# Attention with a bucket mask and two expert layers on one core: when two products of early attention units may be issued

## The chip, the cores and the metric

The program runs on one core of one Trainium2 chip. The metric is the device time of one execution in microseconds; lower is better. The kernel before took 711.56 us, the median of three runs (709.78, 711.56 and 711.82). Its profiled execution took 714.04 us.

## The reference

Attention comes first: two batches, eight heads, 768 positions, head dimension 64. Queries and keys are hashed with six random projections, and a position may only look at positions of its own bucket. Two expert layers follow, each 512 to 2048 to 512.

```
q_bits = (einsum(q, proj) > 0); k_bits = (einsum(k, proj) > 0)     # 6 bits a position
mask   = bucket(q_bits) == bucket(k_bits)
attn   = softmax(where(mask, q @ k.T / sqrt(D), -1e9))
x      = (attn @ v), heads joined                                  # 1536 x 512
h = x @ w_in;  g = where(h > 0, h, exp(min(h, 0)) - 1); x = g @ w_out
h = x @ w_in2; g = s * max(h, 0)**2 + b;                out = g @ w_out2
```

The weights arrive as 64-bit floats and are decoded on the chip. Most products are done with numbers split into a high and a low 16-bit half.

## The kernel before, in words

Attention is cut into 96 units. A unit is 128 query rows of one head against all 768 keys. The first 16 units (two groups of eight, one for each head pair and row chunk) are done in one way, the other 80 in another.

A unit of the first 16 goes through these steps. `u_s` (L384) puts the scores on TensorE in four products into a PSUM tile `s`. `u_soft` (L395 on VectorE, L397 on ScalarE) caps them, takes the smallest of each row and makes the exponentials, the tile `p`. `u_split` (L406) transposes `p` on TensorE into the PSUM tile `pT` by six transposes, and ScalarE copies it to `pt` (L409). `u_av` (L434) multiplies `pt` by the values in six products, which gather in one eighth of the PSUM tile `xacc`. The transposes and these products work on 32-bit floats. There is one buffer for `s`, two for `pT`. A group's eighth unit is followed by `u_norm`, which divides by the sums, splits into halves and transposes by DMA into `x`, the input of the expert layers. The later units split `p` on ScalarE and GpSimd (L416, L419), transpose it by DMA (`pt<-ph`, L421) and multiply in 18 products of 16 bits (L440).

Beside attention two other things run from the start. `w_stream` decodes the first expert layer's weights in 32 chunks of which the 16 of `w_in` come first: a load into one of three buffers `wraw` (L175), then three VectorE instructions L213, L214 and L216, then ScalarE, GpSimd or VectorE for the high and low halves. A load waits until L216 has emptied its buffer. And the four head pairs of the first batch are prepared one after the other: L280 to L315 split and transpose keys and queries, L340 (`pbit`, 18 products) makes the hash bits, L343 turns them into zeros and ones, L353 (`pone`) and L357 turn those into the mask's rows.

When both first groups are done, `moe1` begins with the first expert layer (`h` and `x2p`, L574, products of 128x256), and its products are dealt out between the attention units by a credit. The second batch's keys and queries are loaded when all weights of the first layer have been decoded. The second expert layer (`up2`, `down2`) fills the time from about 475 us.

The code is a list of operations with priorities. A scheduler places them in each engine's queue by its own idea of times, and each engine works through its queue in that order. `tc.issue_after(x)` tells the scheduler not to place the operations under it ahead of the instruction `x`; `pins` is the table of such instructions. A change in one place can thus move instructions on all engines later in the program.

Of the kernel before, what the change touches and what calls it, by code (L numbers as in the profile page):

```python
# [63 lines left out]
W_FROM = 3  # L64
HOLD = {(0, 2, "v"): 3, (0, 3, "v"): 4, (1, 0, "k"): 8, (1, 0, "q"): 9}
HOLD_E = []
LN2 = 0.6931471805599453


def model_kernel(tc, q, k, v, proj, w_in, w_out, w_in2, w_out2, s2, b2, sel, pop, eye, out):  # L70
    nc = tc.nc
# [3 lines left out]
    C = S // 128  # L75
# [19 lines left out]
    with ExitStack() as base:  # L95
# [68 lines left out]
        w_loads, pins = [], {}  # L164

        def behind(n):

            return tc.issue_after(w_loads[n]) if n is not None else nullcontext()
# [9 lines left out]
        def w_early(ch, x):  # L178
            t = xx[1].rearrange("p a t -> p (a t)").bitcast(I32)[:, 1024 * x:1024 * x + 1024]
            with behind(HOLD_E[x]):  # L180
                nc.sync.dma_start(out=t.rearrange("p (k n) -> p k n", k=ch[1].shape[1]), in_=ch[1])
            return ch, t.rearrange("p (n t) -> p n t", t=2)
# [47 lines left out]
        ident = const.tile([128, 128], F32, name="ident")  # L230
# [133 lines left out]
        def unit(u):  # L364
            b, r = divmod(u, C * H)
            c, h = divmod(r, H)
            if u < FC * H:
                c, h = h // (H // 2), H // 2 * c + h % (H // 2)
            return b, c, h, h // 2, h % 2

        def group(u):

            return u // H, u % H
# [4 lines left out]
        def u_s(u):  # L378
            b, c, h, hp, j = unit(u)
            p = ps_s[0].tile([128, S], F32, tag="s", name="s")  # L380
            for x, (w, m) in enumerate(((q1, k1), (q2, k2))):
                kf = m[b, hp][:, j].rearrange("p c t -> p (c t)")
                for a0, a1 in halves:
                    nc.tensor.matmul(p[:, a0:a1], w[b, hp][:, j, c, :], kf[:, a0:a1],  # L384
                                     start=(x == 0), stop=(x == 1))
            sps[u] = p

        def u_soft(u):
# [6 lines left out]
            nc.vector.tensor_scalar(f, sps.pop(u), CLAMP, None, op0=ALU.min, op1=ALU.min, accum_out=mx)  # L395
            (nc.gpsimd if U0 <= u < MXP else nc.vector).tensor_scalar(mx, mx, sm / (SQ * SQ), 10.0 * LN2, op0=ALU.mult, op1=ALU.add)  # L396
            nc.scalar.activation(out=f, in_=f, func=ACTF.Exp, scale=-sm / (SQ * SQ), bias=mx,  # L397
# [3 lines left out]
        def u_split(u, eng):  # L401
            f = pf.pop(u)
            if u < FC * H:
                p = ps_p[0].tile([128, S], F32, tag="s", name="pT")
                for cc in range(C):
                    nc.tensor.transpose(p[:, 128 * cc:128 * cc + 128], f[:, 128 * cc:128 * cc + 128], ident)  # L406
                o = ring.take("pt", [128, S], F32, "pt")
                if eng == "act":
                    nc.scalar.activation(out=o, in_=p, func=ACTF.Copy)  # L409
                else:  # L410
                    nc.vector.tensor_copy(out=o, in_=p)
                pt[u] = o
                return
            t = ring.take("ph", [128, 2, S], F16, "ph")
            if eng == "act":
                nc.scalar.activation(out=t[:, 0, :], in_=f, func=ACTF.Copy)  # L416
            else:
                nc.vector.tensor_copy(out=t[:, 0, :], in_=f)
            nc.gpsimd.tensor_tensor(out=t[:, 1, :], in0=f, in1=t[:, 0, :], op=ALU.subtract)  # L419
            o = ring.take("pt", [128, 2 * C, 128], F16, "pt")  # L420
            nc.sync.dma_start_transpose(out=o, in_=t.rearrange("p x s -> p (x s)"))  # L421
            pt[u] = o

        def u_av(u):
            b, c, h, hp, j = unit(u)
            gr, sl = group(u)
            if sl == 0:
                xacc[gr] = ps_x.tile([128, H, D], F32, tag="x", name="xacc")
            acc = xacc[gr][:, sl, :]
            o = pt.pop(u)  # L430
            if u < FC * H:
                vv = raws[b, hp, "v"].rearrange("p h (c d) -> p h c d", d=D)
                for cc in range(C):
                    nc.tensor.matmul(acc, o[:, 128 * cc:128 * cc + 128], vv[:, j, cc, :],  # L434
                                     start=(cc == 0), stop=(cc == C - 1))
                return
            vv = vHL[b, hp]
            for z, (x, y) in enumerate(((0, 0), (0, 1), (1, 0))):
                for cc in range(C):
                    nc.tensor.matmul(acc, o[:, C * x + cc, :], vv[:, j, cc, y, :],  # L440
                                     start=(z == 0 and cc == 0), stop=(z == 2 and cc == C - 1))
# [76 lines left out]
        def attention():  # L518
            for i in range(-PRE, 0):
                for fn, a in sched.get(i, []):  # L520
                    fn(*a)
                yield
            while nxt["av"] < NU:
                if nxt["split"]:
                    u_split(nxt["split"].pop(0), SPLIT(nxt["s"]))
                u = nxt["av"]
                if u < nxt["s"] and u in pt and (nxt["s"] - u >= nxt["lag"] or nxt["s"] == NU):
                    u_av(u)
                    nxt["av"] += 1
                    if u % H == H - 1:  # L530
                        u_norm(u // H)
                        if u >= FC * H - 1:
                            done_chunks[0] = u // H + 1
                u = nxt["s"]
                if u < NU and u - nxt["av"] < nxt["lag"]:
                    if u == U0:
                        ring.use(p=[unp], ph=[un3], pt=[ptp])
                        nxt["lag"] = PT
                    u_s(u)
                    nxt["s"] += 1  # L540
                    yield
                    u_soft(u)
                    nxt["split"].append(u)
                    for fn, a in sched.get(u, []):
                        fn(*a)
                yield
# [305 lines left out]
        if True:  # L852
# [14 lines left out]
            for _ in att:  # L867
                n += 1
                if len(early) < len(HOLD_E) and len(w_loads) > HOLD_E[len(early)]:
                    early.append(w_early(co1[len(early)], len(early)))  # L870
# [155 lines left out]
```

## Time and profile before

| what | value |
|---|---|
| median of three runs | 711.56 us |
| profiled execution, own time | 714.04 us |
| its span on the core | 711.8 us |
| TensorE busy | 659.6 us, 93% |
| VectorE busy | 520.5 us, 73% |
| ScalarE busy | 416.3 us, 58% |
| GpSimd busy | 266.1 us, 37% |
| mean granted TensorE clock | 0.978 |

The profiled execution's time is 2.2 us longer than its span, and 2.5 us longer than the median of the runs. All instants below are counted from the start of the span. Busy shares are means over stages with different limits: from about 325 us on TensorE is busy almost without a gap, before that it isn't.

### The profile page before, as it was taken

To read this page: it belongs to the slowest core of one execution; us is meant where nothing else is said; L and a number is where in the kernel's file an instruction comes from. 1 tells how busy PE (TensorE), PEld (TensorE's weight loads), DVE (VectorE), ACT (ScalarE), POOL (GpSimd) and SP (SyncE) were. 2 spreads that over 40 slices of the span, in tenths; PEclk is the share of its full clock that TensorE was granted. 3 is DMA by queue.
4 is the path that set the end of the run, shared out by engine and by line. 5 is a ranking of instruction groups with operands and counts; after the bars stand their busy time and mean duration, and the time that the engine had idled before them with its cause. 6 is when DMAs were issued, how large, how long until landed. Compare 5 with 4: busy or idle time off the path is not lost.

```text
span 711.8 us, 15212 instructions
## 1 busy us (share of the span) xinstructions
PE 659.6 (93%) x6192; PEld 506.6 (71%) x6192; DVE 520.5 (73%) x893; ACT 416.3 (58%) x687; POOL 266.1 (37%) x211
## 2 busy tenths in 40 slices
PE   2598978879989999999999999999999999999998
PEld 0286857668767777888888988874444446888887
DVE  5779989998878568645644699339999626999730
ACT  2849768966778788656755333234545525555520
POOL 0136767776345469945855421311211200000000
PEclk9769999999999999999999999999999999999999
DMA  9965699999999669977668555014443000000100
GB/s 211 299 162 170 160 203 203 223 228 225 196 211 216 116 116 171 150 125 122 119 115 117 135 162 165 1 31 119 135 138 112 0 1 1 16 31 31 45 30 30
DMA packets 206805, 89.72 MB, mean 126 GB/s; under 512 B 171920, under 2 KB 203408, under 8 KB 206736
## 3 DMA queue, kind: packets, MB, share of 16 engines
q1 hardware_dynamic: 206144, 88.63, 57.4%
q8 instruction: 48, 0.79, 0.5%
q14 instruction: 21, 0.17, 0.1%
q10 hardware_dynamic: 592, 0.14, 0.1%
HBM read 43.13 MB, written 3.15 MB: 65 GB/s over the span
## 4 chain that ended last, share of the span: by engine, by line
PE 66%; DMA 10%; DVE 10%; ACT 7%; issue 5%; SPq 1%; POOL 1%; DVEq 0%; ACTq 0%; POOLq 0%
PE h L574 27%; PE y L818 15%; PE x2p L574 12%; DMA pt<-ph 6%; PE s L384 4%; PE xacc L440 3%; PE xacc L434 2%; DVE p L395 2%; ACT p L397 1%; PE pT L406 1%; ACT ph L416 1%; DMA q<-src 1%; DVE g L591 1%; DMA raw<-in_k 1%; ACT q L357 1%
## 5 line engine op out<-in xcount | busy, mean ns | idle before, releaser
L419 POOL TENSOR_TENSOR ph<-p,ph 128x768 f16<-128x768 f32 x80 | 134.6, 1686 | 79.2 <-ACT ph L416 44.3
L574 PE MATMUL h<-x,wih 128*128 128x256 f16 x768 | 131.3, 275 | 3.0 <-DVE g L591 1.5
L574 PE MATMUL h<-x,wi 128*128 128x512 f16 x576 | 124.5, 379 | 0.0
L395 DVE TENSOR_SCALAR_CACHE_REDUCE p<-s 128x768 f32<-128x768 f32 x96 | 91.0, 951 | 42.2 <-PE s L384 41.3
L397 ACT ACTIVATE p<-p,mx 128x768 f32<-128x768 f32 x96 | 89.2, 929 | 50.6 <-DVE mx L396 38.8
L818 PE MATMUL y<-wqh,a 128*128 128x256 f16 x672 | 110.3, 273 | 0.0
L818 PEld LDWEIGHTS <-a 128*128 128x128 f16 x1008 | 98.6, 98 | 11.7
L574 PE MATMUL h<-x,wil 128*128 128x256 f16 x384 | 105.4, 275 | 0.0
L574 PE MATMUL x2p<-gh,woh 128*128 128x256 f16 x384 | 104.1, 273 | 0.8 <-ACT gh L594 0.8
L574 PE MATMUL x2p<-gl,woh 128*128 128x256 f16 x384 | 104.5, 273 | 0.1
L574 PEld LDWEIGHTS <-wi 128*128 128x128 f16 x576 | 56.4, 98 | 67.7
L574 PE MATMUL x2p<-gh,wol 128*128 128x256 f16 x384 | 104.5, 273 | 0.0
L818 PE MATMUL y<-wql,a 128*128 128x256 f16 x336 | 91.1, 273 | 0.0
L384 PE MATMUL s<-k,q 128*128 128x512 f16 (+1 forms) x384 | 80.7, 335 | 8.0 <-DVE p L395 7.9
L574 PEld LDWEIGHTS <-wih 128*128 128x128 f16 x768 | 74.9, 99 | 15.2 <-issue 2.0
L574 PEld LDWEIGHTS <-woh 128*128 128x128 f16 x768 | 74.9, 98 | 11.6
L597 POOL TENSOR_TENSOR gl<-g,gh 128x512 f16<-128x512 f32 x48 | 59.0, 1229 | 61.0 <-ACT gh L594 60.7
L440 PE MATMUL xacc<-vv,pt 128*128 128x64 f16 x1440 | 57.6, 194 | 16.1 <-DMA pt<-ph 16.1
L416 ACT ACTIVATE ph<-p 128x768 f16<-128x768 f32 x80 | 66.7, 836 | 7.7 <-DMA pt<-ph 5.2
L440 PEld LDWEIGHTS <-pt 128*128 128x128 f16 x1440 | 53.5, 99 | 24.3 <-DMA pt<-ph 20.3
L610 DVE SCALAR_TENSOR_TENSOR g<-h,sbs,r 128x512 f32<-128x512 f32 x48 | 35.7, 745 | 23.6 <-ACT r L607 23.6
L384 PEld LDWEIGHTS <-q 128*128 128x128 f16 x384 | 34.5, 100 | 25.6 <-issue 10.8
(118 smaller groups left out, 1040.8 us busy)
## 6 DMA issues: line engine op xcount, KB each, us to landing
wraw<-in_moe_w_in SPq DMA_DIRECT2D x32, 512.0 KB, 3.9
wraw<-in_moe_w_out SPq DMA_DIRECT2D x32, 512.0 KB, 3.9
out<-y SPq DMA_DIRECT2D x10, 256.0 KB, 2.0
raw<-in_k SPq DMA_DIRECT2D x6, 384.0 KB, 4.8
raw<-in_q SPq DMA_DIRECT2D x6, 384.0 KB, 5.7
v<-in_v SPq DMA_DIRECT2D x4, 384.0 KB, 7.8
pt<-ph SPq DMA_TRANSPOSE x80, 4.1
x<-in_k SPq DMA_DIRECT2D x2, 384.0 KB, 5.0
```

The costliest lines, as they stand in the source:

```text
L357: nc.scalar.activation(out=o[r, j].rearrange("p c t -> p (c t)"), in_=p[r], func=ACTF.Relu, scale=sc, bias=pop_sb[r, x:x + 1])
L384: nc.tensor.matmul(p[:, a0:a1], w[b, hp][:, j, c, :], kf[:, a0:a1], start=(x == 0), stop=(x == 1))
L395: nc.vector.tensor_scalar(f, sps.pop(u), CLAMP, None, op0=ALU.min, op1=ALU.min, accum_out=mx)
L397: nc.scalar.activation(out=f, in_=f, func=ACTF.Exp, scale=-sm / (SQ * SQ), bias=mx, accum_out=sums[gr][:, sl:sl + 1])
L416: nc.scalar.activation(out=t[:, 0, :], in_=f, func=ACTF.Copy)
L419: nc.gpsimd.tensor_tensor(out=t[:, 1, :], in0=f, in1=t[:, 0, :], op=ALU.subtract)
L434: nc.tensor.matmul(acc, o[:, 128 * cc:128 * cc + 128], vv[:, j, cc, :], start=(cc == 0), stop=(cc == C - 1))
L440: nc.tensor.matmul(acc, o[:, C * x + cc, :], vv[:, j, cc, y, :], start=(z == 0 and cc == 0), stop=(z == 2 and cc == C - 1))
L574: nc.tensor.matmul(p, ws[a](kk), xs[b](kk), start=(kk == 0 and z == 0), stop=(kk == n_kk - 1 and z == 2))
L597: nc.gpsimd.tensor_tensor(out=gl, in0=t["g"], in1=gh, op=ALU.subtract)
L610: nc.vector.scalar_tensor_tensor(out=g, in0=p, scalar=sb["s"], in1=t["r"], op0=ALU.mult, op1=ALU.mult)
L818: nc.tensor.matmul(p, a[:, xa, kk, :], wq[y][:, WQ[n], kk, :], start=first and k == 0, stop=k == 3 * K2 - 1, skip_group_check=True)
```

## The change

Two operations get a place that they may not go ahead of. The first value product of unit 0 is placed behind the last transpose of unit 2, the first value product of unit 1 behind the last score product of unit 4. The other lines only keep these instructions in the table. Each group of six products gathers in one place of PSUM and so follows its first.

```diff
+HOLD_A = {0: ("pT", 2), 1: ("s", 4)}
...
-                    nc.tensor.matmul(p[:, a0:a1], w[b, hp][:, j, c, :], kf[:, a0:a1],
-                                     start=(x == 0), stop=(x == 1))
+                    pins["s", u] = nc.tensor.matmul(p[:, a0:a1], w[b, hp][:, j, c, :], kf[:, a0:a1],
+                                                    start=(x == 0), stop=(x == 1)).ins
...
-                    nc.tensor.transpose(p[:, 128 * cc:128 * cc + 128], f[:, 128 * cc:128 * cc + 128], ident)
+                    pins["pT", u] = nc.tensor.transpose(p[:, 128 * cc:128 * cc + 128], f[:, 128 * cc:128 * cc + 128], ident).ins
...
                 for cc in range(C):
-                    nc.tensor.matmul(acc, o[:, 128 * cc:128 * cc + 128], vv[:, j, cc, :],
-                                     start=(cc == 0), stop=(cc == C - 1))
+                    with tc.issue_after(pins[HOLD_A[u]]) if u in HOLD_A and not cc else nullcontext():
+                        nc.tensor.matmul(acc, o[:, 128 * cc:128 * cc + 128], vv[:, j, cc, :],
+                                         start=(cc == 0), stop=(cc == C - 1))
```

In the changed code the lines behind the first edit are numbered one or two higher: L384 becomes L385, L395 L396, L406 L407, L434 L436, L574 L576.

TensorE's queue before, from the end of unit 3's scores (`s_431`). `pt_317`, `pt_378` and `pt_429` belong to units 0, 1 and 2, `pT_422` and `pT_471` to units 2 and 3, `s_480` is unit 4's scores:

```order
L384 MATMUL s_431<-k21_189,q21_199 128x256
L434 MATMUL xacc_543<-v0_339,pt_317 128x64 x6
L434 MATMUL xacc_543<-v0_339,pt_378 128x64 x6
L406 MATMUL pT_422<-ident_109,p_395 128x128 x6
L384 LDWEIGHTS q10_177
L384 MATMUL s_480<-k10_168,q10_177 128x512
...
L384 MATMUL s_480<-k20_169,q20_179 128x256
L434 MATMUL xacc_543<-v0_400,pt_429 128x64 x6
L406 MATMUL pT_471<-ident_109,p_446 128x128 x6
L340 LDWEIGHTS pjkhl_134
```

The same place now:

```order
L385 MATMUL s_431<-k21_189,q21_199 128x256
L407 MATMUL pT_422<-ident_109,p_395 128x128 x6
L436 MATMUL xacc_543<-v0_339,pt_317 128x64 x6
L385 LDWEIGHTS q10_177
L385 MATMUL s_480<-k10_168,q10_177 128x512
...
L385 MATMUL s_480<-k20_169,q20_179 128x256
L436 MATMUL xacc_543<-v0_339,pt_378 128x64 x6
L436 MATMUL xacc_543<-v0_400,pt_429 128x64 x3
L407 MATMUL pT_471<-ident_109,p_446 128x128 x6
L341 LDWEIGHTS pjkhl_134
```

Unit 2's transposes went ahead of both value products, unit 4's scores ahead of unit 1's. Half of unit 2's value products now stand behind the hash bits and unit 5's scores.

VectorE's queue before, at the reduction of unit 4 (`p_495<-s_480`) and the hash bits of the third head pair (`bits_521`). `wx_327` and `wx_364` belong to two successive weight chunks:

```order
L346 COPY k23_409<-k23_409 64x768
L395 TENSOR_SCALAR p_495,mx_496<-s_480 128x768
L214 SCALAR_TENSOR_TENSOR wx_327<-wraw_288,wx_327 128x512
L396 TENSOR_SCALAR mx_496<-mx_496 128x1
L315 COPY q23_458<-q13_456 64x768 x2
L216 SCALAR_TENSOR_TENSOR wa_326<-wraw_288,wx_327 128x512
L213 TENSOR_SCALAR wx_364<-wraw_308 128x512
L343 TENSOR_SCALAR bits_521<-pbit_500 128x768
L214 SCALAR_TENSOR_TENSOR wx_364<-wraw_308,wx_364 128x512
```

And now:

```order
L347 COPY k23_409<-k23_409 64x768
L215 SCALAR_TENSOR_TENSOR wx_327<-wraw_288,wx_327 128x512
L396 TENSOR_SCALAR p_495,mx_496<-s_480 128x768
L217 SCALAR_TENSOR_TENSOR wa_326<-wraw_288,wx_327 128x512
L316 COPY q23_458<-q13_456 64x768 x2
L397 TENSOR_SCALAR mx_496<-mx_496 128x1
L214 TENSOR_SCALAR wx_364<-wraw_308 128x512
L215 SCALAR_TENSOR_TENSOR wx_364<-wraw_308,wx_364 128x512
L217 SCALAR_TENSOR_TENSOR wa_363<-wraw_308,wx_364 128x512
L344 TENSOR_SCALAR bits_521<-pbit_500 128x768
```

One decoding step now stands ahead of unit 4's reduction, and two more steps of the next chunk (before, behind the bits) stand ahead of the bits.

Later the queues differ too. TensorE's queue before, behind unit 22's scores (`s_1208`), where `h` is the first expert layer:

```order
L384 MATMUL s_1208<-k23_409,q23_458 128x512
L384 LDWEIGHTS q23_458
L384 MATMUL s_1208<-k23_409,q23_458 128x256
L574 LDWEIGHTS wih_154
L574 MATMUL h_1071<-x0_113,wih_154 128x256
```

And now:

```order
L385 MATMUL s_1208<-k23_409,q23_458 128x512
L385 LDWEIGHTS q23_458
L385 MATMUL s_1208<-k23_409,q23_458 128x256
L385 LDWEIGHTS q13_456
L385 MATMUL s_1256<-k13_408,q13_456 128x512
```

Unit 23's scores (`s_1256`) had 36 expert products ahead of them that now come behind. Counted over the whole queue, the expert products (L574) ahead of a unit's scores were 621 and are 591 for unit 48, 792 and 729 for unit 56, and 888 and 888 for unit 67; from there on TensorE's queue is the same in both.

## Rows read from the trace of the kernel before

**Rows 1.** The page, part 1: busy time, share of the span, instructions.
```profile
PE 659.6 (93%) x6192; PEld 506.6 (71%) x6192; DVE 520.5 (73%) x893; ACT 416.3 (58%) x687; POOL 266.1 (37%) x211
```
**Rows 2.** Stretches: length, busy us (count) by engine, granted clock, DMA share, GB/s.
```profile
34.00:49.00 15.00, 15.00 (x79) 12.16 (x78) 9.94 (x20) 6.89 (x12) 5.09 (x4) 0.50 0.87 197
49.00:176.00 127.00, 109.57 (x1168) 88.88 (x1165) 116.95 (x213) 100.33 (x174) 89.73 (x81) 0.97 0.90 197
100.00:275.00 175.00, 156.34 (x1881) 126.57 (x1880) 143.28 (x254) 139.01 (x239) 108.03 (x90) 0.99 0.99 193
205.00:245.00 40.00, 34.27 (x400) 26.50 (x399) 29.50 (x49) 33.44 (x54) 19.51 (x13) 1.00 0.94 177
245.00:275.00 30.00, 28.80 (x366) 23.51 (x365) 20.14 (x47) 25.15 (x43) 21.01 (x15) 1.00 0.77 140
```
**Rows 3.** Timeline of PE, 34 to 56 us: start, length, instructions, idle before, releaser.
```profile
35.69 5.22 PE L434 MATMUL xacc<-v,pt 128*128 128x64 f32 x24
40.70 1.49 PE L406 MATMUL pT<-ident,p 128*128 128x128 f32 x6
41.98 1.49 PE L384 MATMUL s<-k,q 128*128 128x512 f16 x4
43.26 2.66 PE L434 MATMUL xacc<-v,pt 128*128 128x64 f32 x12
45.72 1.49 PE L406 MATMUL pT<-ident,p 128*128 128x128 f32 x6
47.13 0.61 PE L340 MATMUL pbit<-k,pjkhl 128*32 128x512 f16 x2
...
52.32 1.45 PE L434 MATMUL xacc<-v,pt 128*128 128x64 f32 x12
...
55.84 0.81 PE L384 MATMUL s<-k,q 128*128 128x512 f16 x4 [1.42 <-DVE p L395]
```
**Rows 4.** Timeline of DVE, 39 to 50 us.
```profile
39.76 0.36 DVE L346 COPY k<-k 64x768 f16<-64x768 f16 x1
43.51 0.96 DVE L395 TENSOR_SCALAR_CACHE_REDUCE p<-s 128x768 f32<-128x768 f32 x1 [3.39 <-PE s L384]
...
45.18 1.12 DVE L315 COPY q<-q 64x768 f16<-64x768 f16 x2
46.33 0.69 DVE L216 SCALAR_TENSOR_TENSOR wa<-wraw,wx 128x512 int32<-128x512 int32 x1
...
49.18 0.96 DVE L343 TENSOR_SCALAR bits<-pbit 128x768 f16<-128x768 f32 x1 [1.44 <-PE pbit L340]
```
**Rows 5.** Timeline of ACT, 35 to 37 us.
```profile
35.70 0.94 ACT L397 ACTIVATE p<-p,mx 128x768 f32<-128x768 f32 x1 [0.23 <-DVE mx L396]
36.54 0.18 ACT L397 ACTIVATION_READ_ACCUMULATOR p<-p,mx 128x1 f32 x1
```
**Rows 6.** The stretch of one microsecond in which the granted clock rose.
```profile
48.00:49.00 1.00, 1.00 (x16) 0.42 (x8) 0.00 (x0) 0.79 (x2) 0.59 (x1) 0.55 0.73 193
```
**Rows 7.** Waits of DVE, 50 to 180 us: total us, times, longest.
```profile
DVE p L395 <- PE s L384: 5.2, 6, 1.5
DVE g L591 <- ACT e L584: 2.1, 1, 2.1
```
**Rows 8.** Waits of PE, 100 to 320 us.
```profile
PE xacc L440 <- DMA pt<-ph: 14.0, 13, 2.4
```
**Rows 9.** Timelines of DVE and PE at units 53, 56 and 67.
```profile
248.74 0.96 DVE L395 TENSOR_SCALAR_CACHE_REDUCE p<-s 128x768 f32<-128x768 f32 x1 [5.56 <-PE s L384]
252.84 0.81 PE L384 MATMUL s<-k,q 128*128 128x512 f16 x4
276.18 1.46 PE L384 MATMUL s<-k,q 128*128 128x512 f16 x8
```
**Rows 10.** The chain that ended last: start, us, what; an expert product's price.
```profile
178.18 3.63 DMA raw<-in_k
301.56 2.62 PE x2p L574 x24
```

## Prediction

> **What bounds the kernel now.** I read the page's busy shares first: TensorE 93%, VectorE 73% [rows 1]. Such a mean hides stages, so next came the table of stretches [rows 2]. Idle TensorE time is what an early change can win. Of the 175 us from 100 to 275 it is busy for 156.34, so idle for about 18.7 us; 14.0 us of idle time up to 320 us is value products waiting for the transposes by DMA [rows 8]. The stretch from 49 to 176 us belongs to VectorE: 116.95 of 127 us busy. There it decodes weights and does the reductions, and what it gains early it can hand on up to the end of the decoding, which is followed by the second batch's loads, on the chain at 178.18 us [rows 10].
>
> The change acts in 34 to 49 us. Here it is TensorE that has no gap: 15.00 us busy of 15, at a granted clock of 0.50, the lower of the two levels (1.2 GHz) [rows 2]. VectorE works 9.94 us of the 15. Its two waits are both for TensorE: 3.39 us for unit 4's scores and 1.44 us for the hash bits [rows 4]. The reason stands in TensorE's timeline: 24 records of value products for units 0 and 1 run from 35.69 to 40.70 us, 5.01 us, ahead of the transposes and scores on which the other engines wait [rows 3].
>
> **The change part by part.** It removes no instruction and adds none; it reorders. I walk TensorE's queue from 35.69 us with the spacings of [rows 3], all at 1.2 GHz.
>
> Unit 2's transposes come first now, and they need unit 2's exponentials, which ScalarE ends at 36.54 + 0.18 = 36.72 us [rows 5]. So TensorE idles some 1.1 us, until 36.8. Transposes 1.28 us (40.70 to 41.98), to 38.1. Unit 0's products half of 5.01, 2.5 us, to 40.6. Unit 4's scores 1.28 us, to 41.9, against 43.26 before: 1.4 us earlier. Unit 1's products 2.5 us, to 44.4; half of unit 2's products, half of 2.46 us, to 45.6; unit 3's transposes with the step to the bits 1.4 us (45.72 to 47.13), to 47.0. The hash bits begin at 47.0 instead of 47.13. The new gap of 1.1 us is paid by the 1.2 us of unit 2's products that were put behind. Those cost half as much at the higher level: a unit's 12 records take 2.66 us at the one and 1.45 us at the other [rows 3]. For 49 to 56 us that means some 0.6 us more work on TensorE, covered by the 1.42 us that it waits at 55.84 us for VectorE [rows 3]; if that cover went, 0.6 us would be lost.
>
> VectorE's queue in the same time: a decoding step fits behind the copy at 39.76 us, about 0.65 us; the reduction of unit 4 begins near 42.1 instead of 43.51. Behind it stand a decoding step, the copies (1.12 us), and three more decoding steps at 0.69 us each or a little less, since neighbours overlap [rows 4]. The queue is done at about 46.9 us and waits for the bits until 49.05. Waits: 1.4 + 2.2 = 3.6 us where 3.39 + 1.44 = 4.83 us were. The win is two decoding steps done, 1.2 to 1.4 us, plus 0.1 us from the earlier bits. I take 1.5 us of head start. The load buffer emptied by L216 is free near 43.7 instead of 47.0 us, so SP's next weight load goes 3.3 us earlier; SP's queue has nothing in front of it there. I cost it at nothing, since VectorE works on chunks loaded before it; its bounds are the 3.3 us by which it moves, to either side: that much earlier data, or that much delay to the value loads beside which it now runs.
>
> The clock decides how long all this runs at half speed. TensorE was busy without a gap from 34 us on and the clock rose only at about 48.9 (0.55 as the mean of 48 to 49) [rows 6], while the hash bits ran. These come at the same time in both orders, and so I leave the rise where it is. The Trainium skill, "TensorE: Matmul & The Clock Gate", Part 1, says that the moment of release is not the same from run to run, since the monitor isn't tied to the kernel's start; no run here shows that yet. By it, the rise could come earlier or later than 48.9 in either kernel, and neither the sum nor the order of the two changes in the mean. A later rise is priced among the rivals.
>
> What then happens to 1.5 us? From 49 to 176 us VectorE carries it, if its other waits stay: 5.2 us for scores and 2.1 us for an exponential of the expert layer [rows 7]. The second may vanish, since the expert work stands further back in the queue now. So the decoding's end comes 1.5 us earlier, up to 1.5 + 2.1 + 5.2 = 8.8 us at the very most. Behind it the order itself differs: unit 48's scores have 30 expert products less in front of them, unit 56's 63 less, unit 67's none less (counts in the change's section). One costs 2.62 / 24 = 0.109 us [rows 10], so TensorE has 6.9 us less behind it when it reaches unit 56 and makes that up between units 56 and 67. That stretch ran from 252.84 to 276.18 us [rows 9], with TensorE 96% busy, about 0.9 us idle [rows 2]. It will be 23.3 + 6.9 - 0.9 = 29.3 us long. Unit 56 must therefore come 6.0 us earlier just to break even, and 7.5 us earlier for the head start to arrive. For it speak the 5.56 us that VectorE waited at 248.74 for scores that stood behind expert products [rows 9], the ScalarE share of 205 to 245 us (33.44 of 40 us) from which 63 products' worth of activations now go behind, and the head start itself.
>
> Sum: 0 for TensorE up to 49 us, -1.5 us for VectorE handed on, later reordering about even. Against the profiled execution, 714.04 - 1.5 = 712.5 us, its span 711.8 - 1.5 = 710.3; that execution lies 2.5 us above the runs' median, and on the median's scale the forecast is 711.56 - 1.5 = 710.1 us.
>
> **The rivals.**
> *The later queue pays out more.* The waits for scores and for the exponential [rows 7] shrink by half, 3.6 us, and unit 56 comes early enough: 711.56 - 1.5 - 3.6 = 706.5 at the far end, 707.8 with two thirds of it. For it: the waits are for TensorE and ScalarE work that stood behind expert work. Against: TensorE's own waits are mostly for transposes by DMA [rows 8], which no order of products shortens.
>
> *Slower: TensorE starved at units 48 to 56.* The attention there is held by loads, ScalarE and DMA transposes [rows 2, 8], and the expert products that filled the gaps have been put behind. If unit 56 comes only 1.5 us earlier, the end moves by 6.0 - 1.5 = +4.5 us: 716.1. If it comes 4 us earlier: 713.6. It decides from 6.0 us downwards. For it: TensorE was idle 5.7 us of 205 to 245 already. Against: VectorE's long wait above.
>
> *The gap is what counts.* In 34 to 49 us TensorE was the one busy engine, and the change puts a gap of 1.1 us in. If nothing later has slack, 711.56 + 1.1 = 712.7. The Trainium skill, "Perfetto Trace Analysis", Identifying the Most-Contended Engine, reads it so: improve the engine with the most work, by the gaps on it. By that rule the time would be 712.7; the trace speaks against, as TensorE then waits 1.42 us for VectorE at 55.84.
>
> *The clock rises later.* If the low level lasts from 48.9 to the next gap at 54.4, that work, 5.5 us at most, takes twice as long: up to +4 us after the 1.42 us of cover, 715.6.
>
> *No effect.* The head start is used up by another wait, perhaps the loads: 711.6.
>
> **How the numbers follow.** Chances: forecast 0.38 (its own range 708.6 to 711.6), more paid out 0.22, starved 0.23, gap 0.06, clock later 0.04, no effect 0.07. A measurement of this kernel can tell some 0.3%, 2.1 us, from no change: faster is below 709.4, slower above 713.7. Faster: the second case nearly whole, 0.21, and the lower part of the first, 0.15: 0.36. Slower: most of starved, 0.20, of the clock, 0.04, and a little of the gap, 0.02: 0.26. Within: 0.38. Range: down to 706.8, where the second case ends but for some 0.06, and up to 714.8, past the middle of the starved case, with some 0.12 left out.
>
> **What would show it.** Right: unit 4's reduction near 42.1 us, unit 2's transposes at 36.8, the bits at 49.0, VectorE's two waits 3.6 us in sum, the loads of the second batch at 174.5 to 177 instead of 178.18, unit 56's scores at or before 245.4. Wrong: the clock rising anywhere else than about 48.9 us, the second batch's loads no earlier, or unit 56 later than 246.8 us with TensorE idle before it.

## The result: 1.1% slower, and the profile after

| | before | after |
|---|---|---|
| median of 4 runs, us | 711.69 (709.78 to 713.87) | 719.56 (718.15 to 720.40) |
| profiled execution, us: own time, span | 714.04, 711.8 | 719.76, 718.0 |
| TensorE idle in the span, us | 52.2 | 58.1 |

The ratio is 1.0108, with a 95% interval of 1.0074 to 1.0141. The forecast was 710.1 with a range up to 714.8: the sign is wrong. TensorE has the same work (659.6 before, [rows 1]); the span grew by 6.2 us, and its idle time by 5.9.

The page's first part, against [rows 1], and two stretches with the columns of [rows 2]:

```profile
PE 659.9 (92%) x6192; PEld 505.5 (70%) x6192; DVE 527.7 (73%) x893; ACT 415.5 (58%) x687; POOL 264.1 (37%) x211
```
```profile
34.00:49.00 15.00, 11.63 (x92) 9.36 (x91) 13.38 (x24) 8.42 (x14) 6.30 (x6) 0.84 0.98 223
49.00:176.00 127.00, 111.16 (x1145) 89.73 (x1145) 116.27 (x209) 98.58 (x172) 87.53 (x80) 0.92 0.89 193
```

In 34 to 49 us the kernel is faster than foretold. TensorE's timeline there, against [rows 3]:

```profile
36.12 0.88 PE L407 MATMUL pT<-ident,p 128*128 128x128 f32 x6 [0.88 <-ACT p L398]
36.84 1.45 PE L436 MATMUL xacc<-v,pt 128*128 128x64 f32 x12
38.12 0.81 PE L385 MATMUL s<-k,q 128*128 128x512 f16 x4
...
46.56 1.54 PE L407 MATMUL pT<-ident,p 128*128 128x128 f32 x6 [2.07 <-ACT pt L410]
```

Unit 2's transposes come first, behind a gap of 0.88 us, and unit 4's scores stand at 38.12 instead of 41.98. The durations say why this is earlier than the 40.6 that I had worked out: 0.81 us where the scores took 1.49, so the clock was already at its high level. VectorE followed, against [rows 4]:

```profile
42.05 0.96 DVE L396 TENSOR_SCALAR_CACHE_REDUCE p<-s 128x768 f32<-128x768 f32 x1
...
46.79 0.95 DVE L344 TENSOR_SCALAR bits<-pbit 128x768 f16<-128x768 f32 x1
```

Where that lead goes is seen best by the ends of the head groups. VectorE's multiplication xf is a group's last step; here groups 2, 3, 4, 6 and 8 (numbered from 0), before and after:

```profile
125.53 0.68 DVE L462 TENSOR_TENSOR xf<-xacc,rr 128x512 f32<-128x512 f32 x1
153.90 0.69 DVE L462 TENSOR_TENSOR xf<-xacc,rr 128x512 f32<-128x512 f32 x1 [0.19 <-PE xacc L440]
186.30 0.69 DVE L462 TENSOR_TENSOR xf<-xacc,rr 128x512 f32<-128x512 f32 x1
...
267.17 0.68 DVE L462 TENSOR_TENSOR xf<-xacc,rr 128x512 f32<-128x512 f32 x1
...
314.89 0.69 DVE L462 TENSOR_TENSOR xf<-xacc,rr 128x512 f32<-128x512 f32 x1 [0.66 <-PE xacc L440]
```
```profile
119.47 0.69 DVE L464 TENSOR_TENSOR xf<-xacc,rr 128x512 f32<-128x512 f32 x1 [0.25 <-PE xacc L442]
153.94 0.69 DVE L464 TENSOR_TENSOR xf<-xacc,rr 128x512 f32<-128x512 f32 x1 [1.87 <-PE xacc L442]
185.59 0.69 DVE L464 TENSOR_TENSOR xf<-xacc,rr 128x512 f32<-128x512 f32 x1
...
265.70 0.69 DVE L464 TENSOR_TENSOR xf<-xacc,rr 128x512 f32<-128x512 f32 x1 [0.94 <-PE xacc L442]
...
320.68 0.69 DVE L464 TENSOR_TENSOR xf<-xacc,rr 128x512 f32<-128x512 f32 x1 [0.66 <-PE xacc L442]
```

The lead is 6.06 us at group 2, nothing at group 3, 1.47 us at group 6, and at group 8 the changed kernel is 5.79 us behind. From there both need the same time to the end of the span: 711.8 - 314.9 = 396.9 us and 718.0 - 320.7 = 397.3. So two places are suspect: group 3 (119 to 154 us), and groups 7 and 8 (266 to 321 us). Here are three stretches (from the end of group 1 to that of group 4, from 4 to 6, from 6 to 8) as busy time, before and then after; the first number behind the comma is TensorE's, with its count of records, and the granted clock is the number behind POOL's:

```profile
94.14:186.30 92.16, 80.25 (x960) 65.67 (x960) 83.93 (x146) 69.08 (x123) 60.56 (x61) 0.96 1.07 215
186.30:267.17 80.87, 72.61 (x856) 57.75 (x854) 57.93 (x106) 68.37 (x112) 44.00 (x30) 1.00 0.90 168
267.17:314.89 47.72, 46.50 (x607) 39.30 (x605) 30.45 (x71) 34.24 (x60) 38.05 (x26) 1.00 0.93 153
```
```profile
92.03:185.59 93.56, 81.12 (x942) 65.45 (x940) 84.85 (x145) 67.77 (x122) 61.29 (x60) 0.91 1.03 209
185.59:265.70 80.11, 69.23 (x821) 54.04 (x819) 54.56 (x102) 65.92 (x109) 42.65 (x29) 1.00 0.95 173
265.70:320.68 54.98, 52.39 (x659) 44.46 (x658) 38.18 (x74) 36.52 (x66) 38.20 (x26) 1.00 0.74 130
```

The middle stretch has 35 records less on TensorE and is only 0.8 us shorter; the last has 52 more and is 7.3 us longer, 5.9 of it work and 1.4 idle time.

### The profile page after: what moved, and what is told of

Same layout as the page of the kernel before. It is cut to its first block, busy times and chain, and to the rows that moved or that the text cites. A ratio compares the mean times of both kernels' runs of the same rounds, so it can differ in the third digit from the quotient of the medians.

```text
span 718.0 us, 15212 instructions
## 1 busy us (share of the span) xinstructions
PE 659.9 (92%) x6192; PEld 505.5 (70%) x6192; DVE 527.7 (73%) x893; ACT 415.5 (58%) x687; POOL 264.1 (37%) x211
## 4 chain that ended last, share of the span: by engine, by line
PE 57%; ACT 3%; DVE 3%; DMA 1%; issue 1%; POOL 0%; DVEq 0%; ACTq 0%; POOLq 0%
PE h L576 26%; PE y L820 15%; PE x2p L576 11%; PE s L385 3%; PE xacc L442 3%; DMA pt<-ph 1%; DVE e L591 1%; ACT gh L596 1%; ACT p L398 1%; ACT ph L417 1%; DVE g L593 1%; ACT e L584 0%; DVE p L396 0%; ACT k L358 0%; DVE xh L476 0%
## 5 line engine op out<-in xcount | busy, mean ns | idle before, releaser
L420 POOL TENSOR_TENSOR ph<-p,ph 128x768 f16<-128x768 f32 x80 | 132.7, 1665 | 77.1 <-ACT ph L417 49.6
L576 PE MATMUL h<-x,wih 128*128 128x256 f16 x768 | 130.3, 274 | 2.4 <-DMA wraw<-in_moe_w_out 1.3
L576 PE MATMUL h<-x,wi 128*128 128x512 f16 x576 | 124.5, 379 | 0.0
L396 DVE TENSOR_SCALAR_CACHE_REDUCE p<-s 128x768 f32<-128x768 f32 x96 | 91.1, 952 | 42.7 <-PE s L385 41.5
L576 PE MATMUL x2p<-gh,woh 128*128 128x256 f16 x384 | 105.3, 275 | 2.0 <-ACT gh L596 1.6
L576 PE MATMUL x2p<-gl,woh 128*128 128x256 f16 x384 | 105.6, 275 | 1.0 <-POOL gl L599 0.8
L576 PE MATMUL x2p<-gh,wol 128*128 128x256 f16 x384 | 105.6, 275 | 0.0
L576 PE MATMUL h<-x,wil 128*128 128x256 f16 x384 | 105.4, 274 | 0.0
L576 PEld LDWEIGHTS <-wi 128*128 128x128 f16 x576 | 56.4, 98 | 67.7
L385 PE MATMUL s<-k,q 128*128 128x512 f16 (+1 forms) x384 | 80.3, 335 | 9.1 <-DVE p L396 8.8
L576 PEld LDWEIGHTS <-woh 128*128 128x128 f16 x768 | 75.6, 99 | 13.4 <-issue 0.7
L576 PEld LDWEIGHTS <-wih 128*128 128x128 f16 x768 | 74.6, 98 | 14.5 <-issue 3.4
L385 PEld LDWEIGHTS <-q 128*128 128x128 f16 x384 | 34.3, 101 | 27.1 <-issue 12.9
```

The lines of the kernel that those rows point to most:

```text
L385: pins["s", u] = nc.tensor.matmul(p[:, a0:a1], w[b, hp][:, j, c, :], kf[:, a0:a1], start=(x == 0), stop=(x == 1)).ins
L576: nc.tensor.matmul(p, ws[a](kk), xs[b](kk), start=(kk == 0 and z == 0), stop=(kk == n_kk - 1 and z == 2))
```

## The experiments

Theory 1: the order that the scheduler derives behind the change costs the time. Theory 2: the local move does (the gap, and the value sums that are now made in two pieces). Theory 3: the clock does. An interval is of the ratio to runs of the kernel before on the same chip.

**One hold at a time.**

```diff
-HOLD_A = {0: ("pT", 2), 1: ("s", 4)}
+HOLD_A = {0: ("pT", 2)}        # first run
+HOLD_A = {1: ("s", 4)}         # second run
```

> HOLD_A is cut to its first entry: unit 0's value products behind unit 2's transposes; unit 1's are free again. On TensorE's queue the expert products ahead of the scores of every unit from 20 to 70 are as many as in the changed kernel (591 at unit 48, 729 at unit 56, where the kernel before has 621 and 792). Theory 1, the later order costs the time: about the changed kernel's time, 719.5 us (717 to 721). Theory 2, the local move costs it (the gap ahead of unit 2's transposes and the accumulation in pieces): the gap stays and the pieces are fewer, so between the two, 712 to 719 us. Theory 3, the clock between 45 and 55 us: the time follows the granted clock there, 719 if it falls again after 45 us, 713 if not.

> HOLD_A is cut to its second entry: unit 1's value products behind unit 4's scores; unit 0's are free again. The expert products ahead of the later scores come close to the kernel before (618 at unit 48 against 621, 781 at unit 56 against 792). Theory 1, the later order: near the kernel before, 711.5 us (709 to 714). Theory 2, the local move: part of the changed kernel's loss, 713 to 718 us, since unit 4's scores still stand ahead of unit 1's value products. Theory 3, the clock: as in the first, by the granted clock between 45 and 55 us.

Measured: 719.52 us (1.0081 to 1.0165) and 717.65 us (1.0062 to 1.0130). The first hold alone makes the whole loss. The second loses nearly as much, although its product counts ahead of the later scores come close to the old ones: so those counts on TensorE can't be the whole of the order.

**TensorE's scores pinned among the expert products.**

```diff
+ORDER = {23: ([47], [48]), ..., 56: ([791], [792]), ...}
...
+            for u, (ahead_, behind_) in ORDER.items():
+                for n in ahead_:
+                    tc.add_manual_dep(pins["s1", u], prods[n].name, edge, reason="issue_after")
+                for n in behind_:
+                    tc.add_manual_dep(prods[n], pins["s", u].name, edge, reason="issue_after")
```

> The changed kernel with both holds, and the scores of units 23 to 66 pinned between the same two expert products as in the kernel before (621 ahead of unit 48, 792 ahead of unit 56). Only the order of TensorE's queue is pinned. Theory 1, the later order: the whole loss goes, 707 to 713 us; with the lead of 1.5 us that the first stretch gives, 710 as the likeliest. Theory 2, the local move, and theory 3, the clock early in the kernel: the loss stays, 717 to 721 us.

> Both holds are taken out, and the scores of units 23 to 66 are pinned between the same two expert products as in the changed kernel (591 ahead of unit 48, 731 ahead of unit 56). Theory 1, the later order: the loss is there without the change, 717 to 723 us. Theory 2 and theory 3: the time of the kernel before, 710 to 713 us.

Measured: 722.29 us (1.0130 to 1.0195) and 719.98 us (1.0090 to 1.0185). The second is as theory 1 has it: the loss without the change. The first contradicts theory 1 in the form that I gave it: TensorE's scores stand as before among the products, and the kernel is slower still. The pins had left the other rows and the other four queues to the scheduler, so this was half a test. In the traces of these two runs and of the second hold, the stretch from the second batch's loads to the end of group 6 takes 93.3, 94.0 and 93.0 us, against 89.0 before and 87.1 after: part of their loss is another one than the changed kernel's, and no run asks what makes it.

**All five queues pinned.** Each queue's rows were chained one behind the other, up to the last row in which the two kernels differ.

```diff
+ORDER = [...]                  # for each queue its rows, as runs of instruction numbers
...
+            for queue in ORDER:
+                row = [named[f"I-{n0 + d * k}"] for n0, d, num in queue for k in range(num)]
+                for x, y in zip(row[1:], row):
+                    tc.add_manual_dep(x, y.name, edge, reason="issue_after")
```

> The changed kernel with both holds up to about 59 us, and from there the order of the kernel before on all five queues (2291 rows of TensorE, 287 of VectorE, 250 of ScalarE, 122 of GpSimd, 67 of SyncE pinned one behind the other). Theory 1b, the later order of all queues together costs the time, where pinning TensorE's scores alone left the other queues in an order of their own: the loss goes, 707 to 713 us, 710 the likeliest. Theory 2, the local move by itself: the loss stays, 717 to 721 us. Theory 4, the old order fits only the old arrival times: between, 713 to 717 us.

> Both holds are taken out, and from about 59 us on the order of the changed kernel stands on all five queues. Theory 1b: the loss is there without the change, 717 to 722 us. Theory 2, the local move: 709 to 713 us. Theory 4, an order fits only its own arrival times: above the changed kernel, 720 to 725 us.

Measured: 713.39 us, 0.9981 to 1.0027, and 719.41 us, 1.0067 to 1.0151. That settles theory 2: with the change's local move and the old order behind it no loss can be told, and with the new order behind the old walk the whole loss (1.0109 against 1.0108) is there.

**Both kernels traced again.** No edit.

> The kernel before, traced a second time, to tell what changes between two executions of one kernel. Theory 3, the clock decides: if the granted clock of 34 to 49 us is at the high level this time, the time falls by up to 7 us (704 to 707). Theories 1b and 2: 709 to 713 us whatever the clock does in that stretch, since the lead goes in later waits.

> The changed kernel, traced a second time. Theory 3: with the granted clock low in 34 to 49 us this time, up to 5 us longer than 719.8 us. Theories 1b and 2: 718 to 721 us; the waits of 80 to 240 us for the value products' inputs and the clock's falls behind them are there again.

Measured: 709.59 us with a span of 707.4, and 716.49 with 714.7. The granted clock rose at 35 us in the second trace of before, and at 46.7 in that of after. In the first traces it was the other way round, 48.9 and 35. So where the clock rises is not the change's doing. The time of before, 709.59 us, lies in the range of theories 1b and 2 and not in theory 3's 704 to 707; the second trace of after lies below all that was expected of it. What the rise is worth these four traces don't tell: with the early one the span of before is 4.4 us shorter (707.4 against 711.8), but that of after 3.3 us longer (718.0 against 714.7). The rise does not explain the difference between the kernels: the changed kernel's span was 10.6 us longer with the early rise in both, and 2.9 us longer with the late one. The stretch of the last two groups hardly changes between two traces of one kernel: 47.72 and 47.31 us before, 54.98 and 54.99 after. The second trace of after has the loads of the second batch, and the ends of groups 6 and 8, here:

```profile
175.65 0.82 SPq L273 DMA_DIRECT2D raw<-in_k  x1
```
```profile
262.20 0.69 DVE L464 TENSOR_TENSOR xf<-xacc,rr 128x512 f32<-128x512 f32 x1 [0.94 <-PE xacc L442]
...
317.19 0.69 DVE L464 TENSOR_TENSOR xf<-xacc,rr 128x512 f32<-128x512 f32 x1 [0.66 <-PE xacc L442]
```

**The order cut at 177 us.** The same pins, with the one kernel's rows up to the end of the decoding and the other's behind it.

```diff
-ORDER = [...]                  # one kernel's rows
+ORDER = [...]                  # PE rows 0-1219, DVE 0-249, ACT 0-176, POOL 0-99, SP 0-90 of the one, then the other's
```

> The changed kernel's order on all five queues up to the end of decoding (about 177 us; unit 40's scores), and the order of the kernel before behind it. Theory 1b, which part of the later order costs: if the first part (60 to 177 us) costs all of it, 718 to 721 us; if the part behind it does, 710 to 713 us; by the ends of the head groups (group 3 ends 3 to 4 us later than in the old order at the same early clock, the last one 8 to 10 us later) 714 to 716 us.

> The order of the kernel before on all five queues up to about 177 us, and the changed kernel's behind it. First part alone costs: 710 to 713 us. The part behind it alone: 718 to 721 us. By the ends of the head groups: 715 to 717 us, the two parts adding up to the whole 8 us with the run before.

Measured: 712.64 us, 0.9990 to 1.0038, and 718.03 us, 1.0046 to 1.0109. The first suspect is cleared: the new order up to 177 us costs nothing that can be told. The loss is behind it. Old order up to 177 us and new behind, the three stretches:

```profile
89.17:181.52 92.35, 79.70 (x943) 64.65 (x943) 83.75 (x147) 68.62 (x122) 59.74 (x61) 0.94 1.06 214
181.52:261.80 80.28, 72.06 (x821) 55.77 (x819) 52.05 (x103) 66.03 (x109) 42.00 (x29) 0.96 0.92 172
261.80:316.73 54.93, 52.38 (x659) 44.46 (x658) 37.92 (x74) 36.73 (x66) 38.40 (x26) 1.00 0.74 131
```

New order up to 177 us and old behind:

```profile
92.94:184.61 91.67, 80.25 (x950) 64.38 (x948) 83.14 (x144) 68.00 (x123) 60.98 (x60) 0.94 1.07 216
184.61:265.68 81.07, 73.28 (x864) 58.38 (x862) 58.11 (x106) 68.14 (x112) 43.98 (x30) 1.00 0.91 167
265.68:313.15 47.47, 46.65 (x608) 39.55 (x606) 30.26 (x70) 34.36 (x61) 38.39 (x26) 1.00 0.89 154
```

The last stretch goes with the order: 54.93 and 54.98 in the new, 47.47 and 47.72 in the old. The middle one hardly does: 80.28 and 80.11 against 81.07 and 80.87, though the old order has some 35 to 43 records more in it.

**The waits filled.** In the traces of the new order the granted clock falls more often between 80 and 240 us (three to five times, against once or twice), each time behind a wait of 1.6 us or more, though not every such wait is followed by a fall. Idle products keep TensorE busy there.

```diff
+FILL = {18: [(884, 2, 8), (824, 2, 8)], 19: [(846, 3, 9)], 27: [(1225, 3, 16)], ...}
...
+            for at, sl0, times in FILL.get(u, ()):
+                fl = xacc[gr].rearrange("p h d -> p (h d)")[:, D * sl0:]
+                kf = k1[b, hp][:, j].rearrange("p c t -> p (c t)")[:, :D * (H - sl0)]
+                fills[at] = [nc.tensor.matmul(fl, q1[b, hp][:, j, c, :], kf, start=True, stop=True).ins
+                             for _ in range(times)]
```

> The changed kernel's order pinned on all five queues, with 77 idle products set into TensorE's queue right ahead of seven instructions that wait there in every trace of that order: unit 23's scores, unit 18's value products, the expert product behind them, and the value products of units 27, 34, 44 and 48 (they multiply unit's queries and keys into slices of the value sums that the real products overwrite later; 0.13 to 0.21 us each at the high clock, 1 to 2 us per place, less than the wait). Theory 5, the new order's cost is the granted clock, which falls after its longer waits (5.8 to 9.0 us lost that way in 80 to 240 us in the traces of that order, 1.3 to 2.8 us in those of the old one): the falls at 94 to 103, 125, 152, 196 and 222 us go and the time falls to 711 to 716 us. Theory 6, the waits themselves cost and the clock follows them: the time stays at 718 to 721 us, with the clock high.

> The kernel before with its order pinned on all five queues, and 25 idle products set ahead of the scores of units 1 and 2 and the first two units' transposes, where TensorE waits 1.4 to 2.1 us each between 22 and 33 us and the granted clock falls. Theory 5, low clock costs what it takes: the clock stays high through 22 to 49 us, the time falls to 704 to 708 us (the second trace of the kernel before, where the clock rose at 35 us and not at 48 us, has a span 4.4 us shorter). Theory 6, the clock is hidden behind the waits: no change, 710 to 713 us. If the products delay VectorE's reductions: 713 to 716 us.

The first took 722.17 us, 1.0111 to 1.0183. The falls at 125, 152 and 196 us went, those at 94 and 217 stayed, and no time came back. Theory 5 is not borne out for the loss, but not excluded either, since the idle products, 77 of 0.11 to 0.22 us, may have stood in the way of real ones. In the second the fill held: from 20 to 49 us the clock is 1.00, where before it was 0.68 to 34 us, and 0.50 behind [rows 2]; then it fell, from 50.3 to 57.1 us.

```profile
20.00:34.00 14.00, 6.72 (x29) 3.28 (x26) 11.90 (x25) 11.26 (x19) 1.87 (x2) 0.68 1.14 300
```
```profile
20.00:34.00 14.00, 10.57 (x60) 6.03 (x61) 12.54 (x26) 12.15 (x20) 2.71 (x2) 1.00 1.13 303
34.00:49.00 15.00, 12.35 (x109) 9.76 (x109) 14.11 (x28) 9.69 (x15) 6.58 (x5) 1.00 0.89 227
```

709.60 us, ratio 0.9949 to 0.9984: some 0.3% faster than the kernel before, the one version here that beats both. It is above the 704 to 708 of theory 5 and below the 710 of theory 6: part of the low clock was hidden, or came back with the later fall.

**Products moved alone.** TensorE's expert products in the old order are set back, or pulled forward; nothing else on TensorE's queue changes its order. The other queues are pinned to the old order, in the first of the three runs only up to 177 us. The pinned list itself is some 2400 rows long for TensorE; in short form:

```diff
 # product slots of TensorE's old queue: added ahead of a row, taken at and behind a row
+pulled forward: add {1581: 10, 1798: 6, 1872: 10, 1914: 4, 2002: 4}, take {2274: 6, 2315: 6, 2355: 6, 2405: 8, 2442: 8}
+set back: take {1599: 12, 1670: 6, 1741: 12, 1779: 6, 1820: 12, 1934: 9, 1975: 6}, add {2112: 9, 2181: 9, ..., 2405: 9}
```

> The kernel before, pinned on all queues up to about 177 us; behind that TensorE's queue alone is pinned, with 63 expert products moved from ahead of units 48 to 55 to behind unit 57, so that 729 stand ahead of unit 56's scores as in the changed kernel; the other queues are left to the scheduler. Theory 7: the stretch to the end of group 6 stays at 87 to 90 us from the loads, the two groups behind it take 55 instead of 47.7 us, and the time rises by 63 x 0.109 = 6.9 us, 717 to 721 us. Theory 8: no change, 711 to 714 us.

> The kernel before with its order pinned, and 34 expert products pulled ahead of TensorE's waits between 187 and 240 us (10 ahead of unit 44's value products, 6 ahead of unit 47's, 10 ahead of unit 48's, 4 and 4 behind), so that 826 instead of 792 stand ahead of unit 56's scores and 34 fewer behind unit 64. Theory 7, the stretch from the second batch's loads to the end of head group 6 takes its 87 to 90 us whatever number of products stands in it, and a product behind it costs its 0.109 us: the stretch stays, the two groups behind it take 44 instead of 47.7 us, and the time falls by 34 x 0.109 = 3.7 us, 707 to 710 us. Theory 8, TensorE is the bound of that stretch too: it grows by 3.7 us and nothing is gained, 711 to 714 us.

> The same 34 products pulled ahead, with the 25 idle products ahead of the first units' waits as in the run with the filled early waits. Theory 7: both gains add, 2.5 us and 3.7 us under the kernel before, 704 to 707 us. Theory 8: the early fill alone, 708 to 711 us.

Set back: 718.63 us, 1.0080 to 1.0143. That is the size of the loss, and theory 7's 717 to 721. On TensorE nothing but 63 products was moved; on the other queues, which the scheduler arranged anew behind 177 us, some 80 instructions each of VectorE and ScalarE stand elsewhere than before, and no run tells their share. The second and third stretch of this kernel:

```profile
183.74:266.11 82.37, 69.08 (x790) 52.95 (x788) 52.93 (x102) 67.15 (x109) 42.63 (x29) 0.94 0.91 169
266.11:319.29 53.18, 53.10 (x668) 45.45 (x667) 33.21 (x73) 35.71 (x63) 38.55 (x27) 1.00 0.79 132
```

66 records fewer than before stand in the middle, and it is no shorter; TensorE is idle there for 13.29 us instead of 8.26, and the clock falls twice in it (0.94 in the mean). Its waits there for the transposes by DMA went from 5.9 us to 11.4:

```profile
PE xacc L449 <- DMA pt<-ph: 11.4, 6, 3.9
```

The last stretch pays 5.5 us for 61 more; TensorE is busy for 53.10 of its 53.18 us.

Pulled forward: 714.39 us, 1.0025 to 1.0065, slower where theory 7 expected 707 to 710. The traced execution took 712.86 us, less than that median, so its rows can show why nothing was won and not why the median is higher. Its stretches:

```profile
183.73:265.95 82.22, 75.08 (x878) 60.17 (x876) 57.65 (x105) 67.56 (x112) 42.56 (x29) 1.00 0.86 164
265.95:313.67 47.72, 44.28 (x580) 36.63 (x579) 29.94 (x69) 34.87 (x61) 38.83 (x27) 1.00 0.94 155
```

The middle took 22 records more and grew by 1.4 us. The last stretch lost 27 records and is still 47.72 us long. TensorE's waits in it, in the kernel before and here (us in total, times, longest), agree with that:

```profile
PE xacc L440 <- DMA pt<-ph: 1.1, 2, 0.6
```
```profile
PE xacc L449 <- DMA pt<-ph: 3.2, 5, 1.3
```

With fewer products there TensorE waits for the transposed probabilities. So theory 7 holds in one direction alone: in the old order the last stretch is near the bound of both, products more cost their time, and products less save none. Joined with the early fill: 713.10 us, 0.9998 to 1.0040, no gain over the kernel before.

## Why the prediction was wrong

**The local walk** was right in kind, and its gain too small. The gap was 0.88 us for 1.1. In the second trace of the changed kernel, where the clock stayed low up to 46.7 us, nearly as the walk assumed, unit 4's reduction and the bits begin here:

```profile
40.96 0.96 DVE L396 TENSOR_SCALAR_CACHE_REDUCE p<-s 128x768 f32<-128x768 f32 x1 [0.36 <-PE s L385]
...
47.48 0.96 DVE L344 TENSOR_SCALAR bits<-pbit 128x768 f16<-128x768 f32 x1 [1.70 <-PE pbit L341]
```

That is 0.36 + 1.70 = 2.06 us of waits for TensorE where I had 3.6, and the bits 1.5 us ahead of the foretold 49.0. The walk also lacked a wait of 1.14 us for a copy's data at 39.51 us.

**The clock's rise, left at 48.9 us,** was a chance of one trace. Two traces of one kernel differ by 14 us. The rule that I cited from the Trainium skill, "TensorE: Matmul & The Clock Gate", Part 1, that the moment of release varies from run to run, is borne out; the half a microsecond that the page gives for it is not.

**The lead handed on** came out in part. In the old order the second trace of before leads the first by 4.1 us at group 4 (182.2 for 186.3), by 4.7 at group 8 (310.2 for 314.9) and by 4.4 at the end. With the new walk and the old order the span is 709.2, 2.6 us less than the first trace of before, which also had the late rise; that fits 1.5 us or a little more. The timed ratio of 0.9981 to 1.0027 can't tell it from nothing. In the new order it depends on the trace. In the first one the second batch's loads came at 178.60 us against 178.18 in [rows 10], where I foretold 174.5 to 177. In the second, with the late rise as in the first trace of before, they came at 175.65, as foretold; there the changed kernel is 5.0 us ahead at group 6 (262.20 for 267.17), 2.3 us behind at group 8 (317.19 for 314.89) and 2.9 us at the end. So a lead arrives, and what loses it is the stretch of the last two groups.

**The later order about even: this step failed.** I had the right kind of sum, 63 products x 0.109 = 6.9 us to be made up, 6.0 us after the idle time, and then let unit 56 come early enough to pay for it. It came 3.04 us earlier, by TensorE's timelines of before and of after:

```profile
255.90 0.81 PE L384 MATMUL s<-k,q 128*128 128x512 f16 x4
```
```profile
252.86 0.81 PE L385 MATMUL s<-k,q 128*128 128x512 f16 x4
```

(The row at 252.84 us that I took for unit 56 in [rows 9] is unit 55's, and the one at 276.18 us, which I took for unit 67, holds units 65 and 66. Unit 67's scores begin at 280.72 us before and 285.62 after. So the stretch from unit 56 to 67 was 24.8 us long and became 32.8: 7.9 us more, where I had 6.0.) My first reason was VectorE's wait of 5.56 us for scores [rows 9], which I put down to the products in front of them. They are unit 52's scores, and 56 of the 748 products ahead of them went. VectorE waits all the same, 3.94 us for these and 1.67 for unit 53's, 5.61 us where it was 5.56 + 0.98 = 6.54:

```profile
246.12 0.96 DVE L396 TENSOR_SCALAR_CACHE_REDUCE p<-s 128x768 f32<-128x768 f32 x1 [3.94 <-PE s L385]
...
248.95 0.96 DVE L396 TENSOR_SCALAR_CACHE_REDUCE p<-s 128x768 f32<-128x768 f32 x1 [1.67 <-PE s L385]
```

Unit 52's scores also need the mask's rows, which ScalarE writes into the key tile (`k<-pone`). Before, these were done at 246.46 us and the scores stood at 247.80, so products that still stood in front can have held them up by 1.3 us at most; now the scores begin as soon as the rows are there:

```profile
244.65 1.81 ACT L357 ACTIVATE k<-pone,pop_sb 64x768 f16<-64x768 f32 x2
247.80 0.81 PE L384 MATMUL s<-k,q 128*128 128x512 f16 x4
```
```profile
245.18 0.81 PE L385 MATMUL s<-k,q 128*128 128x512 f16 x4 [0.27 <-ACT k L358]
```

For the most part the products had been filling time that the scores had to wait for anyway. From the second batch's loads to the end of group 6 it takes 89.0 us before (178.18 to 267.17), 87.1 after (178.60 to 265.70), 90.0 with 63 products fewer (176.06 to 266.11), 89.7 with 34 more (176.25 to 265.95); in the second traces it is 89.1 before and 86.6 after. Of the 6.9 us taken out there some 2.5 are saved at most, and behind it the products cost their whole time.

**The rival "TensorE starved"** named this mechanism and its point of decision, and had 0.23. By its formula unit 56's 3.0 us would have given +3.0; the end moved by 6.2. The last two groups became 7.3 us longer, not 6.0, since 1.4 us of idle time came on top, and of unit 56's lead only 1.5 us were left at group 6's end. The gap was no cost that can be told: the run with all later queues in the old order has it, 1.08 us, at a ratio of 0.9981 to 1.0027.

**Left open** is which engine paces the 87 to 90 us from the loads to group 6. From group 4 to 6 ScalarE is busy for 68.37 of 80.87 us before, and of TensorE's 10.9 us of idle time after the change 6.0 are waits for transposes by DMA; no run took either away. Open too is what the clock's later falls cost by themselves.

## What to carry to other kernels

Work that is taken out of a stretch saves time there only if its engine paces the stretch; otherwise it was filler, and it costs its whole time where it lands if its engine is busy throughout there. Before a move is called even, add up from the trace how long the stretch takes at the least without the work, by two traces if there are two, and not by one long wait that stands behind it. And where a scheduler answers a local edit with another order everywhere, pin all queues to the old order first: here that showed that the edit itself was worth nothing that can be told, either way.

## What the hardware showed beside

Nearly equal idle time left the granted clock unequal. From 80 to 160 us TensorE was busy 66.82 us at a mean clock of 0.98 in the second trace of before, and 67.64 us at 0.94 in that of after. In these traces the new order has fewer and longer waits, the old one more and shorter ones. One place, unit 27's value products in the new order and the nearest wait in the old, with the ten microseconds around it:

```profile
124.66 0.70 PE L442 MATMUL xacc<-vv,pt 128*128 128x64 f16 x18 [2.80 <-DMA pt<-ph]
```
```profile
120.00:130.00 10.00, 7.20 (x62) 5.26 (x61) 8.95 (x16) 6.06 (x11) 7.70 (x9) 0.83 1.21 230
```
```profile
126.08 0.70 PE L440 MATMUL xacc<-vv,pt 128*128 128x64 f16 x18 [1.07 <-DMA pt<-ph]
```
```profile
120.00:130.00 10.00, 8.01 (x99) 6.63 (x99) 9.96 (x18) 8.65 (x17) 7.23 (x9) 1.00 1.09 234
```

After the wait of 2.80 us the clock was at the low level for some 3.4 us; after the wait of 1.07 us it stayed high. The length of the wait alone doesn't decide it. One instruction in the two traces of the kernel before, the first and the second:

```profile
160.17 0.70 PE L440 MATMUL xacc<-vv,pt 128*128 128x64 f16 x18 [2.36 <-DMA pt<-ph]
```
```profile
155.84 0.70 PE L440 MATMUL xacc<-vv,pt 128*128 128x64 f16 x18 [2.38 <-DMA pt<-ph]
```

In the first the clock was low from 161.5 to 165.0 us, in the second it stayed high. And the rise is no matter of a gap alone: in the first trace of before TensorE had no gap from 34 us on and worked nearly 15 us at the low level [rows 2], while with idle products ahead of 34 us the high level held until 50.3 us.
